# Attention and two expert layers on one core: two weight-preparation steps per projection unit, and a 32-byte pad at the right edge of SBUF

## The chip, the cores and the metric

The program runs on one core of a Trainium2 chip. The metric is the device time of one execution in microseconds (us); the kernel before has a median of 1267.8 us over three runs (1267.17 to 1268.67).

## What is computed

```
rmsnorm(x, g) = x / sqrt(mean(x*x) + 1e-6) * g            # over head_dim
attn = softmax(rmsnorm(q) @ rmsnorm(k).T / sqrt(64)) @ v    # batch 4, 12 heads, 448 positions, head_dim 64
x    = attn laid out as 1792 tokens x 768
h    = max(x @ w_in, 0);   x = (h*h) @ w_out                # d_ff 2048
g    = x @ w_gate;         out = (silu(g) * (x @ w_val)) @ w_out2     # d_ff 1536
```

All weights arrive as float64 and are read by the kernel as pairs of 32-bit words.

## The kernel before, in words

**Three stages.** `attention()` walks over 24 pairs of heads; `moe()` then runs phase 0 (`w_in`, `w_out`) and phase 1 (`w_gate`, `w_val`, `w_out2`). The order of work on every engine is the order in which the code issues it (`tc.manual_schedule()`): each engine takes its own queue strictly in that order.

**Precision.** Every operand of the two expert layers is split into a high part (cast to fp32r) and a low part (the rest), and each product takes three matmuls: high times high, weight high times activation low, weight low times activation high.

**Units.** The 1792 tokens are four blocks t = 0 to 3 of 448. The list `units` (L669 to L686) orders the expert layers. A *projection unit* P(f,t) multiplies a slab of 128 hidden columns with block t of the activations: 18 matmuls of 128x448 on TensorE (L610) in phase 0, 36 in phase 1, reading the activation tile `xs0` to `xs3` of that block. Its result is finished on two engines, in `up`: ScalarE takes the relu (L631), VectorE the square (L632), ScalarE casts the high part of `hid` (L171), VectorE subtracts for the low part (L172). An *output unit* O(t) multiplies the two `hid` slabs f = 0 and f = 1 of a group with `w_out`: six accumulators of six matmuls each (L658), whose first three read `hid0` (f = 0) and whose last three read `hid` (f = 1); VectorE adds each accumulator to `xacc` (L666, in the first group a copy, L664). After the first group the order within a group g is

```
P00  O3 of g-1  P01  P02  P03  P10  P11  O0  P12  O1  P13  O2
```

so five projection units stand in a row, and O0, which reads the `hid` of P10, comes one unit after it.

**Weight preparation.** `pieces()` turns each slab of weights from float64 words into an fp32r high and low part, in six steps, in the text named A to F; `prep(n)` at the head of each unit (L691) issues the next n of them, before the unit's own work:

- A: a shift on VectorE (L135) and a square on ScalarE (L139)
- B: VectorE, L141
- C: VectorE, L145; the raw buffer is then free, and the next unit issues the load of a later slab on SyncE
- D: VectorE, L150
- E: ScalarE casts the high part (L154), from what D wrote
- F: VectorE subtracts for the low part (L156), from what E wrote

A ring of six prepared slabs (`NSLOT`) bounds how far preparation may run ahead: with a full ring a step is a no-op. A group of phase 0 needs four slabs, 24 steps, and has eight projection units and four output units.

**Memory.** Pools grow from the left or from the right edge of SBUF. On the left stand `xs0`, `xs1`, the weight ring `w0` to `w5`, `hid0`, `hid` and `xacc`. At the right edge (`side="right"`) stand in the attention `th`, `p`, `sg`, `v`, `nm`, `ones`, `onef`, `xu`, `rb` and others, and later `xs2` and `xs3` (pool `xb`). In the built program the left tiles begin at multiples of 64 bytes in their partition (`xs0` 44736, `xs1` 66240, `hid0` 147136, `hid` 161472 and 165568), those at the right edge all at 32 past a multiple of 64 (`xs2` 173536, `xs3` 195040, `th` 155808). A row of 448 fp32 numbers is 1792 bytes, 28 times 64.

Of the kernel before, what the change touches and what calls it, by code (L numbers as in the profile page):

```python
# [8 lines left out]
F32 = mybir.dt.float32  # L9
# [10 lines left out]
def kernel(  # L20
# [17 lines left out]
    P = 128  # L38
# [11 lines left out]
    NB = len(blocks)  # L50

    const = ctx.enter_context(tc.tile_pool(name="const", bufs=1))

    ident = const.tile([P, P], F32, name="ident")
    make_identity(nc, ident)
# [53 lines left out]
    def load_slabs():  # L109
        while state["want"]:  # L110
            state["want"] -= 1
            load_slab()
# [51 lines left out]
    def prep(n=1):  # L164
        for _ in range(n):
            next(steps, None)
# [7 lines left out]
    def split_hi(t, kk):  # L174
        b0, n = blocks[t]
        nc.scalar.copy(xs[t][:, 0, kk, :], x[:, kk, b0:b0 + n])

    def split_lo(t, kk, eng=nc.vector):
        b0, n = blocks[t]
        eng.tensor_tensor(  # L180
            out=xs[t][:, 1, kk, :], in0=x[:, kk, b0:b0 + n], in1=xs[t][:, 0, kk, :].bitcast(F32), op=ALU.subtract
        )
# [409 lines left out]
    def moe():  # L592
# [32 lines left out]
        def up(g, f, t):  # L625
            b0, n = blocks[t]
            ps = psp.tile([P, 512], F32, tag="ps", name="ps")
            proj(ps, ("in", g, f), t)
            hh, hl = hidden(f, t)
            s = scr.tile([P, 512], F32, tag="s", name="s")  # L630
            nc.scalar.activation(out=s[:, :n], in_=ps[:, :n], func=AF.Relu)  # L631
            nc.vector.tensor_tensor(out=s[:, :n], in0=ps[:, :n], in1=s[:, :n], op=ALU.mult)  # L632
            split(hh, hl, s[:, :n])

        def gateval(g, f, t):
            b0, n = blocks[t]
            pg = psp.tile([P, 512], F32, tag="ps", name="ps")
            proj(pg, ("gate", g, f), t)
            hh, hl = hidden(f, t)
            s = scr.tile([P, 512], F32, tag="s", name="s")  # L640
            nc.scalar.activation(out=s[:, :n], in_=pg[:, :n], func=AF.Sigmoid)  # L641
            nc.vector.tensor_tensor(out=s[:, :n], in0=pg[:, :n], in1=s[:, :n], op=ALU.mult)  # L642
            pv = psp.tile([P, 512], F32, tag="ps", name="ps")
            proj(pv, ("val", g, f), t)
            nc.vector.tensor_tensor(out=s[:, :n], in0=pv[:, :n], in1=s[:, :n], op=ALU.mult)  # L645
            split(hh, hl, s[:, :n])

        def down(name, g, t, last):
            b0, n = blocks[t]
            hd = hid_t.pop(t)  # L650
            for o in range(KD):
                ps = psp.tile([P, 512], F32, tag="ps", name="ps")
                mm = 0
                for f in range(2):
                    w = W[(name, g, f)]
                    for wi, hi in ((0, 0), (0, 1), (1, 0)):
                        rhs = hid0[:, hi, b0:b0 + n] if f == 0 else hd[:, hi, :n]
                        nc.tensor.matmul(  # L658
                            ps[:, :n], w[:, wi, o * P:(o + 1) * P], rhs, start=(mm == 0), stop=(mm == 5)
                        )  # L660
                        mm += 1
                a = acc[:, o, b0:b0 + n]
                if g == 0:
                    nc.vector.tensor_copy(a, ps[:, :n])  # L664
                else:
                    nc.vector.tensor_tensor(out=a, in0=ps[:, :n], in1=a, op=ALU.add)  # L666
                if last and name == "out":
                    split(xs[t][:, 0, o, :], xs[t][:, 1, o, :], a, nc.gpsimd)
                elif last:  # L669
                    nc.sync.dma_start(out=out[o * P:(o + 1) * P, b0:b0 + n], in_=a)  # L670
# [17 lines left out]
        for i, (phase, kind, g, f, t) in enumerate(units):  # L688
            state["freed"] = freed
            load_slabs()  # L690
            prep(2 if i < 2 else 1 if i < 7 else 3 if phase == 0 else 4 if kind else 5)  # L691
            while drain and drain[0][0] == i:
                _, fn, arg = drain.pop(0)
                fn(arg)
            endt = t == NB - 1
            if phase == 0 and kind == 0:
                up(g, f, t)
                freed += endt
            elif phase == 0:
                down("out", g, t, g == DFF // 256 - 1)  # L700
                freed += 2 * endt
            elif kind == 0:
                gateval(g, f, t)
                freed += 2 * endt
            else:
                down("out2", g, t, g == DFF2 // 256 - 1)
                freed += 2 * endt
            for t, kk in (
                ((2, 0),), ((2, 1), (2, 2)), ((2, 3), (2, 4)), ((2, 5), (3, 0)), ((3, 1), (3, 2)), ((3, 3), (3, 4)), ((3, 5),)
            )[i] if i < 7 else ():  # L710
                split_hi(t, kk)
                split_lo(t, kk, nc.gpsimd if kk % 2 == 1 else nc.vector)

    with tc.manual_schedule():
        attention()
        moe()
# [31 lines left out]
```

## Time and profile before

| what | before |
|---|---|
| median of 3 runs | 1267.8 us |
| the profiled execution's own time | 1267.85 us |
| its span, first to last instruction | 1266.1 us |
| TensorE busy | 1252.4 us (99%) |
| VectorE busy | 826.6 us (65%) |
| ScalarE busy | 432.7 us (34%) |
| GpSimd busy | 250.0 us (20%) |
[...]

Busy time of TensorE counts a matmul from its start to its modelled end, and neighbours overlap; so how fast a stream of matmuls runs is read from the distance of their starts, and small waits hide inside the busy time. In a row of the timeline, "start, length, xN" is a run of N instructions without another kind between them. For matmuls that follow each other the distance of two starts is the length less one matmul's own duration (0.367 us), divided by N-1.

### The profile page before, as it was taken

How to read it: one execution, taken by the hardware profiler on the slowest of the kernel's cores; microseconds unless marked ns; L12 is line 12 of the kernel's file. 1: busy time of each engine (PE TensorE's matmuls, PEld its weight loads, DVE VectorE, ACT ScalarE, POOL GpSimd, SP SyncE). 2: the span in 40 equal slices, each digit the busy share in tenths (PEclk: the TensorE clock that was granted, in tenths of full speed). 3: DMA queues.
4: the chain of work that ended last, by engine and by line, in shares of the span. 5: the costliest groups of instructions: out<-in, count | busy, mean ns of one | idle time of the engine just before them, and what ended most of it. 6: DMA issues, size and time to landing. Idle time of an engine off the chain costs nothing.

```text
span 1266.1 us, 16840 instructions
## 1 busy us (share of the span) xinstructions
PE 1252.4 (99%) x6766; PEld 1064.8 (84%) x6766; DVE 826.6 (65%) x1168; ACT 432.7 (34%) x679; POOL 250.0 (20%) x268
## 2 busy tenths in 40 slices
PE   8999999999999999999999999999999999999998
PEld 5555555589898989898999999999999999999998
DVE  6777777767767676766767665565665664765634
ACT  5777777643313131222222432121221230221210
POOL 3889999630000000000000540000000000000000
PEclk9999999999999999999999999999999999999999
DMA  4433332131212021111112111111120220220013
GB/s 124 145 116 97 114 98 56 45 95 50 76 50 76 26 75 42 59 51 50 50 50 75 51 51 50 49 52 50 50 75 25 75 76 1 77 74 26 25 44 131
DMA packets 64830, 82.35 MB, mean 65 GB/s; under 512 B 8176, under 2 KB 61168, under 8 KB 64752
## 3 DMA queue, kind: packets, MB, share of 16 engines
q1 hardware_dynamic: 64432, 81.28, 20.6%
q8 instruction: 53, 0.87, 0.3%
q14 instruction: 25, 0.20, 0.1%
q10 hardware_dynamic: 320, 0.00, 0.0%
HBM read 75.50 MB, written 5.59 MB: 64 GB/s over the span
## 4 chain that ended last, share of the span: by engine, by line
PE 86%; DVE 7%; ACT 4%; POOL 2%; issue 1%; DMA 0%; ACTq 0%; POOLq 0%; DVEq 0%
PE ps L610 38%; PE ps L658 32%; PE s L365 5%; PE s L380 4%; PE s L336 2%; PE s L401 1%; DVE hid L172 1%; PE s L306 1%; ACT hid L171 1%; DVE s L632 1%; DVE bits L150 1%; DVE w L156 1%; ACT w L154 1%; POOL sg L371 1%; POOL qk L288 1%
## 5 line engine op out<-in xcount | busy, mean ns | idle before, releaser
L610 PE MATMUL ps<-xs,w 128*128 128x448 f32 x2880 | 598.0, 367 | 0.7 <-ACT sb L409 0.7
L610 PEld LDWEIGHTS ps<-xs,w 128*128 128x128 f32 x2880 | 541.0, 188 | 49.1 <-ACT sb L409 1.5
L658 PE MATMUL ps<-hid,w 128*128 128x448 f32 x2016 | 421.2, 366 | 2.3 <-DVE hid L172 1.3
L658 PEld LDWEIGHTS ps<-hid,w 128*128 128x128 f32 x2016 | 378.0, 188 | 36.8 <-DVE hid L172 3.5
L666 DVE TENSOR_TENSOR xacc<-ps,xacc 128x448 f32<-128x448 f32 x288 | 167.5, 619 | 53.1 <-PE ps L658 51.5
L171 ACT CAST hid<-s 128x448 fp32r<-128x448 f32 x112 | 63.5, 567 | 235.3 <-DVE s L645 160.8
L339 DVE TENSOR_REDUCE mxz<-s 112x2 f32<-112x896 f32 x96 | 101.2, 1092 | 24.4 <-PE s L336 23.6
L172 DVE TENSOR_TENSOR hid<-s,hid 128x448 fp32r<-128x448 f32 x112 | 70.1, 626 | 70.9 <-ACT hid L171 70.9
L172 POOL TENSOR_TENSOR xs<-xacc,xs 128x448 fp32r<-128x448 f32 x24 | 29.0, 1248 | 425.3 <-ACT xs L171 425.3
L154 ACT CAST w<-bits 128x768 fp32r<-128x768 f32 x68 | 56.7, 834 | 149.4 <-DVE bits L150 149.4
L371 POOL TENSOR_TENSOR sg<-p 112x896 f32<-112x896 f32 x46 | 97.7, 2125 | 11.8 <-ACT p L367 9.9
L367 ACT ACTIVATE p<-s 112x896 f32<-112x896 f32 x96 | 87.1, 919 | 14.6 <-PE s L365 11.2
L156 DVE TENSOR_TENSOR w<-bits,w 128x768 fp32r<-128x768 f32 x68 | 65.0, 956 | 32.2 <-ACT w L154 30.9
L641 ACT ACTIVATE s<-ps 128x448 f32<-128x448 f32 x48 | 26.1, 544 | 165.6 <-PE ps L610 165.6
L631 ACT ACTIVATE s<-ps 128x448 f32<-128x448 f32 x64 | 34.7, 542 | 136.3 <-PE ps L610 136.3
L365 PE MATMUL s<-th 64*112 64x448 f32 x576 | 76.9, 371 | 2.8 <-ACT p L367 1.4
L645 DVE TENSOR_TENSOR s<-ps,s 128x448 f32<-128x448 f32 x48 | 30.0, 625 | 73.6 <-PE ps L610 72.8
L380 PE MATMUL s<-p,v 112*64 112x448 f32 x384 | 77.5, 545 | 0.0
L642 DVE TENSOR_TENSOR s<-ps,s 128x448 f32<-128x448 f32 x48 | 29.9, 622 | 72.8 <-ACT s L641 72.8
L139 ACT ACTIVATE w<-raw 128x768 fp32r<-128x768 f32 x68 | 61.7, 907 | 45.5 <-PE ps L658 45.5
L632 DVE TENSOR_TENSOR s<-ps,s 128x448 f32<-128x448 f32 x64 | 39.7, 620 | 50.7 <-ACT s L631 50.7
L145 DVE SCALAR_TENSOR_TENSOR bits<-raw,bits 128x768 int32<-128x768 int32 x68 | 66.7, 980 | 2.0
(64 smaller groups left out, 832.6 us busy)
## 6 DMA issues: line engine op xcount, KB each, us to landing
raw<-in_moe_w_out_dram SPq DMA_DIRECT2D x28, 768.0 KB
raw<-in_moe_w_in_dram SPq DMA_DIRECT2D x16, 768.0 KB
raw<-in_moe_w_gate_dram SPq DMA_DIRECT2D x12, 768.0 KB
raw<-in_moe_w_val_dram SPq DMA_DIRECT2D x12, 768.0 KB
raw<-in_k_dram SPq DMA_DIRECT2D x24, 224.0 KB
raw<-in_q_dram SPq DMA_DIRECT2D x24, 224.0 KB
v<-in_v_dram SPq DMA_DIRECT2D x24, 224.0 KB
rb<-row SPq DMA_DIRECT2D x48, 112.0 KB
```

The source lines that it names most:

```text
L154: nc.scalar.copy(t[:, 0, :], src)
L156: nc.vector.tensor_tensor(out=t[:, 1, :], in0=src, in1=t[:, 0, :].bitcast(F32), op=ALU.subtract)
L171: nc.scalar.copy(dh, src)
L172: (eng or nc.vector).tensor_tensor(out=dl, in0=src, in1=dh.bitcast(F32), op=ALU.subtract)
L339: nc.vector.tensor_reduce(out=mxz[:, c, 0:P:D], in_=ps[:CP, :, :S], op=ALU.max, axis=AX.X)
L365: nc.tensor.matmul(ps[:CP, a, :S], lhs, rhs, start=(w == 0), stop=(w == 3))
L367: nc.scalar.activation(out=p, in_=ps[:CP, :, :S], func=AF.Exp)
L371: nc.gpsimd.tensor_tensor(out=sg, in0=p_t[pi, 2 * w], in1=p_t[pi, 2 * w + 1], op=ALU.add)
L380: nc.tensor.matmul(ps[s, :S], v_t[pi][:, a, c * D:(c + 1) * D], p[:, a, :], start=(c == 0), stop=(c == NCH - 1),)
L610: nc.tensor.matmul(ps[:, :n], w[:, wi, kk, :], xs[t][:, xi, kk, :], start=(mm == 0), stop=(mm == 3 * KD - 1))
L658: nc.tensor.matmul(ps[:, :n], w[:, wi, o * P:(o + 1) * P], rhs, start=(mm == 0), stop=(mm == 5))
L666: nc.vector.tensor_tensor(out=a, in0=ps[:, :n], in1=a, op=ALU.add)
```

## The change

It adds a pool `edge` with one tile of eight fp32 numbers (32 bytes in each partition) as the first at the right edge, so that every tile behind it there begins 32 bytes lower: `xs2` at 173504, `xs3` at 195008, `th` at 155776, all multiples of 64. The tile is never written or read. And in phase 0, from unit 7 on, `prep` gives two steps at a projection unit (`kind` 0) and still three at an output unit (`kind` 1).

```diff
     const = ctx.enter_context(tc.tile_pool(name="const", bufs=1))
+
+    edge = ctx.enter_context(tc.tile_pool(name="edge", bufs=1, side="right"))
+    edge.tile([P, 8], F32, name="pad")
...
             load_slabs()
-            prep(2 if i < 2 else 1 if i < 7 else 3 if phase == 0 else 4 if kind else 5)
+            prep(2 if i < 2 else 1 if i < 7 else 2 + kind if phase == 0 else 4 if kind else 5)
```

No instruction is added or taken away on any engine; the steps of preparation move along the queues of VectorE and ScalarE, with the loads of SyncE behind them. Line numbers in the change are three higher. The numbers in the names of `w` and `hid` are buffer counts; `hid_...` with a number is `hid0`, and `hid` alone is the f = 1 tile.

VectorE before, group 2 of phase 0: from step F ahead of P02 to the low part of P10. The row `hid<-s,hid` is the low part of P10, which O0 waits for.

```order
L156 TENSOR_TENSOR w_4307<-bits,w_4307 128x768
L632 TENSOR_TENSOR s<-ps,s 128x448
L172 TENSOR_TENSOR hid_3361<-s,hid_3361 128x448
L135 TENSOR_SCALAR bits<-raw 128x768
L141 SCALAR_TENSOR_TENSOR bits<-raw,bits 128x768
L145 SCALAR_TENSOR_TENSOR bits<-raw,bits 128x768
L632 TENSOR_TENSOR s<-ps,s 128x448
L172 TENSOR_TENSOR hid_3361<-s,hid_3361 128x448
L150 SCALAR_TENSOR_TENSOR bits<-w_4366,bits 128x768
L156 TENSOR_TENSOR w_4366<-bits,w_4366 128x768
L632 TENSOR_TENSOR s<-ps,s 128x448
L172 TENSOR_TENSOR hid<-s,hid 128x448
```

VectorE in the change, the same group, from step B ahead of P02 to the low part of P10:

```order
L144 SCALAR_TENSOR_TENSOR bits<-raw,bits 128x768
L148 SCALAR_TENSOR_TENSOR bits<-raw,bits 128x768
L635 TENSOR_TENSOR s<-ps,s 128x448
L175 TENSOR_TENSOR hid_3365<-s,hid_3365 128x448
L153 SCALAR_TENSOR_TENSOR bits<-w_4311,bits 128x768
L635 TENSOR_TENSOR s<-ps,s 128x448
L175 TENSOR_TENSOR hid_3365<-s,hid_3365 128x448
L159 TENSOR_TENSOR w_4311<-bits,w_4311 128x768
L138 TENSOR_SCALAR bits<-raw 128x768
L635 TENSOR_TENSOR s<-ps,s 128x448
L175 TENSOR_TENSOR hid<-s,hid 128x448
```

Ahead of P10's two operations stood D and F, with E between them on the other engine; now F of a slab and A of the next stand there, and D and E have moved to P03.

ScalarE before, the same stretch: P03 (with A ahead of it), P10 (with E ahead of it), P11 (with A).

```order
L139 ACTIVATE w_4366<-raw 128x768
L631 ACTIVATE s<-ps 128x448
L171 CAST hid_3361<-s 128x448
L154 CAST w_4366<-bits 128x768
L631 ACTIVATE s<-ps 128x448
L171 CAST hid<-s 128x448
L139 ACTIVATE w_4426<-raw 128x768
L631 ACTIVATE s<-ps 128x448
L171 CAST hid<-s 128x448
```

ScalarE in the change: P03 (with E ahead of it), P10 (with A), P11 (with nothing).

```order
L157 CAST w_4311<-bits 128x768
L634 ACTIVATE s<-ps 128x448
L174 CAST hid_3365<-s 128x448
L142 ACTIVATE w_4394<-raw 128x768
L634 ACTIVATE s<-ps 128x448
L174 CAST hid<-s 128x448
L634 ACTIVATE s<-ps 128x448
L174 CAST hid<-s 128x448
```

The relu of P10 stood behind a cast that waits for D of the same unit; now it stands behind a square that waits for a raw slab alone.

## Rows read from the trace of the kernel before

**Rows 1.** Page: busy time of the engines, and the granted clock in 40 slices
```profile
PE 1252.4 (99%) x6766; PEld 1064.8 (84%) x6766; DVE 826.6 (65%) x1168; ACT 432.7 (34%) x679; POOL 250.0 (20%) x268
...
PEclk9999999999999999999999999999999999999999
```

**Rows 2.** Page, the chain that ended last, share of the span by engine
```profile
PE 86%; DVE 7%; ACT 4%; POOL 2%; issue 1%; DMA 0%; ACTq 0%; POOLq 0%; DVEq 0%
```

**Rows 3.** Busy time by stretch: 21 attention rounds, one round, expert layers, two groups
```profile
core 0: us, PE busy (x) PEld busy (x) DVE busy (x) ACT busy (x) POOL busy (x), PEclk, DMA share, GB/s
37.83:245.69 207.86, 205.39 (x1589) 117.79 (x1588) 158.23 (x189) 156.97 (x244) 186.06 (x193) 1.00 0.34 99
226.31:236.00 9.69, 9.69 (x78) 5.62 (x77) 6.89 (x8) 6.61 (x11) 6.30 (x7) 1.00 0.17 50
258.78:1266.10 1007.32, 1001.50 (x4896) 919.05 (x4896) 636.10 (x937) 246.89 (x390) 41.82 (x37) 1.00 0.17 56
440.94:500.26 59.32, 59.13 (x289) 54.02 (x288) 40.02 (x60) 15.26 (x25) 0.00 (x0) 1.00 0.17 54
1027.62:1115.72 88.10, 88.10 (x434) 81.16 (x433) 53.77 (x78) 18.46 (x28) 0.00 (x0) 1.00 0.17 54
```

**Rows 4.** Who waited for whom, TensorE, phase 0 (260 to 705 us): total, times, longest
```profile
PE ps L658 <- DVE hid L172: 1.3, 7, 0.2
PE ps L658 <- ACT hid L171: 1.0, 1, 1.0
```

**Rows 5.** Timeline of TensorE at O0 of group 2: start, us, instructions
```profile
400.00 1.21 PE L658 MATMUL ps<-hid,w 128*128 128x448 f32 x4
401.40 1.89 PE L658 MATMUL ps<-hid,w 128*128 128x448 f32 x8 [0.19 <-DVE hid L172]
```

**Rows 6.** Timeline of TensorE at O0 of group 1
```profile
339.60 0.77 PE L658 MATMUL ps<-hid,w 128*128 128x448 f32 x3
341.34 0.47 PE L658 MATMUL ps<-hid,w 128*128 128x448 f32 x1 [0.97 <-ACT hid L171]
342.00 3.36 PE L658 MATMUL ps<-hid,w 128*128 128x448 f32 x15 [0.19 <-DVE hid L172]
```

**Rows 7.** Timeline of VectorE, group 2, from P03's preparation to P10's low part
```profile
392.43 0.55 DVE L135 TENSOR_SCALAR bits<-raw 128x768 int32<-128x768 int32 x1
393.01 0.96 DVE L141 SCALAR_TENSOR_TENSOR bits<-raw,bits 128x768 int32<-128x768 int32 x1
394.01 0.96 DVE L145 SCALAR_TENSOR_TENSOR bits<-raw,bits 128x768 int32<-128x768 int32 x1
394.88 0.62 DVE L632 TENSOR_TENSOR s<-ps,s 128x448 f32<-128x448 f32 x1
396.13 0.62 DVE L172 TENSOR_TENSOR hid<-s,hid 128x448 fp32r<-128x448 f32 x1 [0.63 <-ACT hid L171]
396.67 0.95 DVE L150 SCALAR_TENSOR_TENSOR bits<-w,bits 128x768 f32<-128x768 f32 x1
398.59 0.96 DVE L156 TENSOR_TENSOR w<-bits,w 128x768 fp32r<-128x768 f32 x1 [0.96 <-ACT w L154]
399.47 0.62 DVE L632 TENSOR_TENSOR s<-ps,s 128x448 f32<-128x448 f32 x1
400.72 0.62 DVE L172 TENSOR_TENSOR hid<-s,hid 128x448 fp32r<-128x448 f32 x1 [0.63 <-ACT hid L171]
```

**Rows 8.** Timeline of ScalarE, group 2: P01's relu, then P10 with E ahead
```profile
385.47 0.55 ACT L631 ACTIVATE s<-ps 128x448 f32<-128x448 f32 x1 [3.35 <-PE ps L610]
...
397.72 0.84 ACT L154 CAST w<-bits 128x768 fp32r<-128x768 f32 x1 [1.62 <-DVE bits L150]
398.46 0.54 ACT L631 ACTIVATE s<-ps 128x448 f32<-128x448 f32 x1
400.12 0.57 ACT L171 CAST hid<-s 128x448 fp32r<-128x448 f32 x1 [1.12 <-DVE s L632]
```

**Rows 9.** Timeline of TensorE, 72 matmuls of xs2 and xs3 (phase 1)
```profile
1012.75 15.03 PE L610 MATMUL ps<-xs,w 128*128 128x448 f32 x72
```

**Rows 10.** The same, the 72 matmuls of xs0 and xs1 that follow
```profile
1027.62 14.76 PE L610 MATMUL ps<-xs,w 128*128 128x448 f32 x72
```

**Rows 11.** The same, the 36 matmuls of hid0 and hid behind those
```profile
1042.21 7.46 PE L658 MATMUL ps<-hid,w 128*128 128x448 f32 x36
```

**Rows 12.** Timeline of TensorE, one attention round: first and last pair of scores
```profile
229.77 0.76 PE L365 MATMUL s<-th 64*112 64x448 f32 x6
...
233.51 0.37 PE L365 MATMUL s<-nm,ones 64*112 64x448 f32 x2
```

**Rows 13.** ScalarE's casts into xs0 to xs3 after phase 0: ns min/median/max
```profile
L171 ACT CAST xs<-xacc x24: 566/568/571, 705.5 to 742.1; 128x448 fp32r<-128x448 f32 x24
```

## The prediction
> **What bounds the kernel now.** First the page: TensorE is busy for 1252.4 us of 1266.1, at the full granted clock in every slice, and the chain that ended last lies on it for 86%; the other 14% are worth finding, because half of them are VectorE's [rows 1, 2]. Then the stretches: the expert layers take 1007 us with 4896 matmuls of one shape, the attention the rest [rows 3]. Then the timeline of TensorE, from which the distance between two matmuls comes: it shows two things.
>
> *One shape, two speeds.* 72 matmuls that read xs2 and xs3 take 15.03 us [rows 9]: less the last one's own 0.37 us and divided by 71, that is 206.5 ns each. The 72 behind them, same weights of the same ring and same shape, but reading xs0 and xs1, take 14.76 us [rows 10]: 202.7 ns. The 36 that read hid0 and hid are at 7.46 us [rows 11], (7.46 - 0.37) / 35 = 202.6 ns. xs2 and xs3 are the ones that stand 32 bytes past a multiple of 64.
>
> *A wait once in a group of phase 0.* A group has 288 matmuls, 72 of them on xs2 and xs3. 216 x 202.7 + 72 x 206.5 ns = 58.65 us, but it took 59.32 us [rows 3]: 0.67 us are lost. In phase 1 the same sum, 288 x 202.7 + 144 x 206.5 ns = 88.11 us, meets 88.10 [rows 3]: nothing is lost there. The loss of phase 0 is at O0: seven waits for the low part of hid and one long one for its high part [rows 4]. At 400.00 O0 begins; its fifth matmul should start 4 x 0.203 = 0.81 us later and starts at 1.40, and the next eight take 1.89 us where 7 x 0.203 + 0.37 = 1.79 are due [rows 5]: 0.59 + 0.10 = 0.69 us. In group 1 it is more: the fourth matmul starts at 341.34 in place of 340.21, the fifth 0.66 us after it in place of 0.20, and the start-up behind that costs the same 0.10 [rows 6]: 1.13 + 0.46 + 0.10 = 1.69 us.
>
> **Why O0 waits.** P10's matmuls end 3.65 us (18 x 202.7 ns) before O0 begins, at 396.35. P11 and P10 at 3.65 us and P03 and P02 at 3.72 (18 x 206.5 ns), counted back from 400.00, put the ends of P03, P02 and P01 at 392.70, 388.98 and 385.26. In P01, where nothing was queued ahead, the relu began 0.2 us after that, at 385.47 [rows 8]. For P10 it began at 398.46, 2.1 us after the end, because ScalarE had the cast E ahead of it, E waited for D, and D had waited behind the low part of P03 [rows 7, 8]. VectorE then did F before the square. From the relu's start the chain is relu 0.55, square 0.62, cast 0.57, low part 0.62 us plus 0.03 between them, about 2.45 us when nothing is in its way; here it ended at 401.34. With three steps a projection unit gives VectorE either A, B, C (0.55 + 0.96 + 0.96, to 2.5 us with the gaps) or D, E, F, which crosses to ScalarE and back (0.95 + 0.84 + 0.96, 2.9 us with the gaps), on top of 1.9 us from the start of its square to the end of its low part: 4.4 to 4.8 us where TensorE takes 3.65 to 3.72. Over five projection units in a row the two engines fall behind, and O0 is where it shows.
>
> **The change, part by part.**
>
> *Steps, term 1.* Moved: one step of each projection unit in phase 0; nothing is added. I carry the timetable of group 2 forward on the times of before. P01's low part is as before, to 387.93. P02 now has B, C on VectorE, to 389.87; its relu (matmuls end 388.98) is done by then, so square to 390.50, cast to 391.10, low part to 391.75. P03 has D to 392.75, E on ScalarE to 393.65; its relu, due at 392.90, comes behind E and ends at 394.20; square to 394.85, cast 395.45, low part 396.10. P10 has F, A on VectorE, to 397.65; ScalarE did the square of A at 395.5 to 396.4, so the relu starts at its due 396.55 and ends 397.10; square to 398.30, cast 398.90, low part 399.55. O0 first reads the high part at 400.61 and the low part at 400.81: it is there 1.3 us early, where before it was 0.5 us late. The other groups differ in which steps fall on P03 and P10. From group 3 on (E, F and A, B; the same work, and no D directly ahead of E) the slack is 1.5 us or more; in group 1 (F, A and B, C) I get the low part 3.0 us after P10's matmuls end, with 4.25 allowed. So all seven waits go: 1.69 + 6 x 0.69 = **5.8 us**.
>
> What moves with it: what was prepared ahead of projection units is now partly done at output units and at units where a full ring made steps no-ops. An output unit lasts 36 x 0.203 = 7.3 us and asks VectorE for six additions of 0.62 us and three steps of at most 2.9: 6.6 us, covered. Supply is 8 x 2 + 4 x 3 = 28 steps for the 24 that a group needs, so preparation does not starve. Counting steps along the units, the narrowest lead is the second w_out slab of group 1: finished in P03, read at O0, three units or 11 us later (before: five); in later groups of the phase five or more. Loads: C is later, and so is each load issued after it on SyncE, but a slab's A comes nine steps behind its load's issue, some four projection units; nothing else of weight is in SyncE's queue in this phase, and the traffic is 54 GB/s [rows 3]. GpSimd is idle there. Cost: nothing, as long as that lead stands.
>
> *Pad, term 2, expert layers.* 1440 matmuls read xs2 and xs3 (16 projection units of 18 in phase 0, 576; 24 of 36 in phase 1, 864). If the 32 bytes are what makes them slow, each falls from 206.5 to 202.7 ns: 1440 x 3.8 = **5.4 us**, all on the path, since TensorE has no other wait there. Before does not show xs2 or xs3 at another address, so the bounds are 0 and 5.4; I take 5.4, because xs0, xs1, hid0 and hid, five address ranges that share nothing but the alignment, all run at 202.7. A loss I exclude by the same rows. Writing the moved tiles costs ScalarE the same: its casts into xs0 to xs3 all take 566 to 571 ns [rows 13].
>
> [...]
>
> *Pad, term 3, attention.* A round has 20 pairs of 64-row matmuls on th and nm. 18 of their distances lie between 229.77 and 233.51 [rows 12]: 207.8 ns each, nearest to the slow rate of xs2. At 3.8 ns less each, 20 x 24 rounds = 480 pairs give 1.8 us. The other matmuls on moved tiles (p, sg) have another form; granting them the same 3.8 ns for some 12 pairs a round adds 1.1, so the bounds are 0 and 2.9 us. The undisturbed round is 9.69 us, the mean of 21 is 207.86 / 21 = 9.90 [rows 3]: in part of the rounds another engine's wait ends last and would eat the gain. I take half of 1.8: **0.9 us**. The warm-up and the tail hold no such stream.
>
> **Sum.** 1267.85 us, the profiled execution (the median of 1267.8 is the same within the runs' spread) - 5.8 - 5.4 - 0.9 = 1255.75, so **1255.8 us**, 0.95% less. Its own range is 1253.3 (attention at 2.9, less 0.5 for the spread of runs) to 1257.5.
>
> **The rivals.**
>
> - *The pad does nothing.* [...] For it: no row separates address from alignment. Against it: five left-hand ranges at one speed. Terms 2 and 3 go: 1267.85 - 5.8 = 1262.1 us. Chance 0.10.
> - *The wait at O0 stays in part.* VectorE's queue is denser than my timetable, for instance because step A of one slab waits for its load, or F for E behind a relu; 1.3 us of delay in P10 brings the first part of the wait back. Half of it left gives 1258.7, all of it 1261.6 us. Against it: the timetable has 1.2 to 1.5 us to spare in every group. Chance 0.07.
> - *Preparation comes too late.* The mechanism on the slow side: a projection or output unit reaches a slab whose F has not been done, and TensorE waits for VectorE and ScalarE at the first matmul of the slab. It decides once the lead of three units, 11 us, is used up, and pays when the waits are over 12.1 / 7 = 1.7 us in each of seven groups; at one projection unit (3.7 us) in each it gives 1255.8 + 26 = 1282 us. Against it: 28 steps against 24 needed. Chance 0.03.
> - *No change.* The pad does nothing and the waits move to O1 or O2 at the same length: 1267.8 us. Against it: O1 and O2 have 11 us between their hid and its use. Chance 0.02.
>
> **How the numbers follow.** The forecast has 0.78. 8 times in 10: the forecast's own range, and of the second rival the part up to half of the wait: 1253.3 to 1260.0; the pad that does nothing, at 1262.1, is left out with its 0.10. A measurement of this kernel tells about 0.2%, 2.5 us, from no change. Faster by more than that are the forecast and the first two rivals, 0.95; within it 0.02; slower 0.03.
>
> **What would show it.** In the changed profile: a stretch of 72 matmuls on xs2 and xs3 in 14.76 us like xs0 and xs1 (if 15.03, term 2 is wrong); no wait of TensorE for hid in phase 0, and a group of phase 0 in 288 x 202.7 ns = 58.4 us in place of 59.32; a group of phase 1 in 87.6 in place of 88.10; the undisturbed attention round at 9.6 in place of 9.69, and the start of the expert layers about 0.9 us earlier than 258.78 (if it moves by over 2 us, term 3 is too small). A wait of TensorE for `w` in phase 0 would be the third rival.

## The result, and the profile after

The changed kernel takes 1257.5 us (median of 5 runs) against 1268.4 us for the kernel before on the same chip: ratio 0.9905, 95% interval 0.9892 to 0.9919. The forecast was 1255.8 us with a range of 1253.3 to 1260.0. One thing must be known to read the numbers: of 17 executions of the changed kernel 7 took 1255.7 to 1257.5 us and 10 took 1275.4 to 1280.3, longer than the kernel before, and the ratios go by the 7. The profile that came with the result is of an execution of 1276.34 us; that of `again`, which is the change unaltered, is of one of 1257.0 us. Both profiles are needed. The lines below answer to [rows 1] and [rows 2]; the first fence is the page of the 1276.34 us execution, the second that of the 1257.0 us one (span, busy time of the engines, the chain that ended last by engine).

```profile
span 1274.5 us, 16838 instructions
...
PE 1262.5 (99%) x6766; PEld 1064.4 (84%) x6766; DVE 828.5 (65%) x1168; ACT 433.6 (34%) x679; POOL 251.7 (20%) x268
...
PE 92%; POOL 2%; DMA 2%; DVE 1%; ACT 1%; issue 1%; SPq 0%; POOLq 0%; ACTq 0%; DVEq 0%
```

```profile
span 1255.2 us, 16838 instructions
...
PE 1243.6 (99%) x6766; PEld 1065.7 (85%) x6766; DVE 826.8 (66%) x1168; ACT 433.2 (35%) x679; POOL 251.6 (20%) x268
...
PEclk9999999999999999999999999999999999999999
...
PE 93%; POOL 2%; DMA 1%; DVE 1%; ACT 1%; issue 1%; SPq 0%; POOLq 0%; ACTq 0%; DVEq 0%
```

In both, VectorE's share of the chain has fallen from 7% to 1% and ScalarE's from 4% to 1%: the waits at O0 are gone from either execution. The instructions are the same. What differs between the two is TensorE's busy time, by 18.9 us, at a granted clock of 1.000 and 0.999; no other engine's differs by more than 2 us.

The stretches of the 1257.0 us execution, which answer to [rows 3] (same columns: from:to and length, busy time by engine, clock, DMA): start to the expert layers, expert layers, group 3 of phase 0 (from its P01 to the P01 of the next group), a group of phase 1, one attention round.

```profile
0.00:259.23 259.23, 251.07 (x1870) 146.04 (x1870) 190.78 (x231) 185.59 (x289) 208.59 (x231) 1.00 0.35 100
259.23:1255.20 995.97, 992.52 (x4896) 919.63 (x4896) 636.06 (x937) 247.65 (x390) 43.01 (x37) 1.00 0.18 57
438.09:496.46 58.37, 58.37 (x290) 54.10 (x288) 39.62 (x60) 15.39 (x25) 0.00 (x0) 1.00 0.17 55
1018.12:1105.67 87.55, 87.55 (x433) 81.15 (x432) 53.76 (x78) 18.46 (x28) 0.00 (x0) 1.00 0.17 55
226.44:236.15 9.71, 9.71 (x77) 5.67 (x77) 6.90 (x8) 6.60 (x11) 6.08 (x6) 1.00 0.18 50
```

The gain lies in the expert layers and nowhere else: they begin at 259.23 in place of 258.78 us, and the 4896 matmuls of that stretch are busy for 992.52 in place of 1001.50 us. The same group of phase 0 takes 58.37 in place of 59.32 us, one of phase 1 87.55 in place of 88.10.

The timelines of TensorE that answer to [rows 9], [rows 10] and [rows 11] (start, us, instructions): 72 matmuls on xs2 and xs3, 72 on xs0 and xs1, 36 on hid0 and hid. First `again`, 1257.0 us:

```profile
1003.53 14.76 PE L613 MATMUL ps<-xs,w 128*128 128x448 f32 x72
1018.12 14.75 PE L613 MATMUL ps<-xs,w 128*128 128x448 f32 x72
1032.71 7.46 PE L661 MATMUL ps<-hid,w 128*128 128x448 f32 x36
```

The same three places of the execution of 1276.34 us:

```profile
1017.94 15.04 PE L613 MATMUL ps<-xs,w 128*128 128x448 f32 x72
1032.82 15.04 PE L613 MATMUL ps<-xs,w 128*128 128x448 f32 x72
1047.70 7.60 PE L661 MATMUL ps<-hid,w 128*128 128x448 f32 x36
```

With the pad, all moving tiles run alike in both executions. In the one the distance between matmuls is (14.76 - 0.37) / 71 = 202.7 ns, in the other (15.04 - 0.37) / 71 = 206.6 ns, and so through the whole stream: (15.04 - 14.76) / 71 = 3.94 ns, and 4896 x 3.94 ns = 19.3 us, which is the difference of the two times. Term 2 of the prediction came true at the first distance and was lost several times over at the second. Why that is so was the question for the experiments.

### The profile page after: what moved, and what is told of

It reads as the page before. It is cut to its first block, busy times and chain, and to the rows that moved or that the text cites. A ratio compares the mean times of both kernels' runs of the same rounds, so it can differ in the third digit from the quotient of the medians.

```text
span 1274.5 us, 16838 instructions
## 1 busy us (share of the span) xinstructions
PE 1262.5 (99%) x6766; PEld 1064.4 (84%) x6766; DVE 828.5 (65%) x1168; ACT 433.6 (34%) x679; POOL 251.7 (20%) x268
## 4 chain that ended last, share of the span: by engine, by line
PE 92%; POOL 2%; DMA 2%; DVE 1%; ACT 1%; issue 1%; SPq 0%; POOLq 0%; ACTq 0%; DVEq 0%
PE ps L613 47%; PE ps L661 33%; PE s L368 5%; PE s L383 4%; PE s L339 2%; PE s L404 1%; PE s L309 1%; POOL sg L374 1%; POOL qk L291 1%; DMA raw<-in_k_dram 1%; PE s L348 0%; DMA v<-in_v_dram 0%; ACT sq L252 0%; DMA rb<-row 0%; DVE ss L259 0%
## 5 line engine op out<-in xcount | busy, mean ns | idle before, releaser
L613 PE MATMUL ps<-xs,w 128*128 128x448 f32 x2880 | 604.2, 368 | 0.7 <-ACT sb L412 0.7
L661 PE MATMUL ps<-hid,w 128*128 128x448 f32 x2016 | 425.5, 368 | 0.0
L174 ACT CAST hid<-s 128x448 fp32r<-128x448 f32 x112 | 63.5, 567 | 207.8 <-DVE s L648 162.4
```

The costliest lines, as they stand in the source:

```text
L174: nc.scalar.copy(dh, src)
L613: nc.tensor.matmul(ps[:, :n], w[:, wi, kk, :], xs[t][:, xi, kk, :], start=(mm == 0), stop=(mm == 3 * KD - 1))
L661: nc.tensor.matmul(ps[:, :n], w[:, wi, o * P:(o + 1) * P], rhs, start=(mm == 0), stop=(mm == 5))
```

## The experiments

Eleven runs follow, two of them of a kernel that had run already, all beside runs of the kernel before on the same chip, whose medians lay between 1267.8 and 1268.6 us. That a tile stands "at 64" means that its byte address in its partition is 64 modulo 128; "against the weights" is a moving tile's address less that of the weight ring (the first pool of slabs), modulo 128. In the kernel before, the ring, xs0, xs1, hid0 and hid stand at 64 and xs2, xs3 at 96. The change puts xs2 and xs3 at 64 too.

### The two parts, each alone

`again` is the change without an edit, and is told above.

> The changed kernel unaltered, for a profile of an undisturbed execution and for more times. Theory 1 (a 448-column row that begins 32 bytes past a multiple of 64 costs a matmul 3.8 ns, and the pad removes that): about 1255.8 us, all six moving tiles (xs0 to xs3, hid0, hid) at 202.7 ns from start to start, no wait at O0. Rival (the address range, not the alignment, makes xs2 and xs3 slow): about 1262 us, xs2 and xs3 still at 206.5 ns, the rest at 202.7.

Measured: ratio 0.9906 (0.9893 to 0.9919), the same as the first time.

`steps_only` leaves the pad out:

```diff
-            prep(2 if i < 2 else 1 if i < 7 else 3 if phase == 0 else 4 if kind else 5)
+            prep(2 if i < 2 else 1 if i < 7 else 2 + kind if phase == 0 else 4 if kind else 5)
```

> The two steps alone, without the pad. Both theories: no wait at O0 in any group, xs2 and xs3 at 206.5 ns, the rest at 202.7: 1267.85 - 5.8 = 1262.1 us. If the waits move instead of going, nearer to 1267.

Measured: 1262.1 us, ratio 0.9957 (0.9941 to 0.9973), and TensorE has no wait at O0. Group 3 of this kernel, by stretch:

```profile
439.62:498.25 58.63, 58.63 (x290) 54.10 (x288) 39.65 (x60) 15.37 (x25) 0.00 (x0) 1.00 0.17 54
```

58.63 us is what 216 x 202.7 + 72 x 206.5 ns make, 58.65: the 0.67 us that [rows 3] lost are back, and xs2 and xs3 are as slow as before. From the start of the first to the start of the last matmul of the expert layers the kernel before takes 1262.24 - 258.78 = 1003.46 us, this one 1257.49 - 259.96 = 997.53: 5.93 us less. Term 1 stands by itself.

`pad_only` has the pad and keeps three steps:

```diff
+    edge = ctx.enter_context(tc.tile_pool(name="edge", bufs=1, side="right"))
+    edge.tile([P, 8], F32, name="pad")
```

> The pad alone, three steps at each projection unit as before. Theory 1: the wait at O0 stays (5.8 us in seven groups), xs2 and xs3 fall to 202.7 ns: 1267.85 - 5.4 - 0.9 = about 1261.5 us. Rival (address range): 1267.8 us, no change.

Measured: 1264.8 us, ratio 0.9968 (0.9957 to 0.9979): between the two expectations. Its timeline of TensorE shows why. The rows are: group 2, xs2 and xs3, then xs0 and xs1, then O0 with its wait; and 59 us later the same pairs of tiles in group 3.

```profile
387.81 7.60 PE L613 MATMUL ps<-xs,w 128*128 128x448 f32 x36
395.25 7.60 PE L613 MATMUL ps<-xs,w 128*128 128x448 f32 x36
402.69 1.03 PE L661 MATMUL ps<-hid,w 128*128 128x448 f32 x4
403.92 1.89 PE L661 MATMUL ps<-hid,w 128*128 128x448 f32 x8 [0.19 <-DVE hid L175]
...
446.99 7.46 PE L613 MATMUL ps<-xs,w 128*128 128x448 f32 x36
454.29 7.46 PE L613 MATMUL ps<-xs,w 128*128 128x448 f32 x36
```

Ahead of the wait at O0 every tile is at (7.60 - 0.37) / 35 = 206.6 ns, behind it every tile is at 202.6. Nothing but the wait lies between. So both rates that the changed kernel shows in different executions stand here in one: with xs and hid at the same place the stream has **two rates**, keeps the one that it is in, and a wait can move it to the other. Not every wait does: in this execution the one at O0 of group 1 left the stream at 206.7, and those of groups 3 to 7 left it at 202.7. The seven waits for VectorE at O0 are still there, as in [rows 4]:

```profile
PE ps L661 <- DVE hid L175: 1.3, 7, 0.2
PE ps L661 <- ACT hid L174: 0.8, 1, 0.8
```

The stretch at 206.6 ns, from 260 to 403 us, is 143 / 0.2067 = 690 matmuls x 4 ns, 2.8 us above what the expectation with the pad took. That is for this execution, of 1266.34 us; another 0.9 us of the miss is term 3, which did not come.

No execution of `pad_only` took 1276 us: all seven lie between 1264.3 and 1266.3. The change has no wait at O0, and in its execution of 1276.34 us every unit, from the first to the last, ran at 206.6 to 206.7 ns. So the two parts seem to lean on each other: the steps also take away the waits that can end a stretch at the slower rate. One trace shows such an end; the other six executions have none.

### Is it the rows' own alignment?

`left_off` has two steps, no pad at the right edge, and the same 32 bytes at the left edge instead, so that the ring, xs0, xs1, hid0 and hid all move to 96, where xs2 and xs3 stand:

```diff
+    shift = ctx.enter_context(tc.tile_pool(name="shift", bufs=1))
+    shift.tile([P, 8], F32, name="pad")
```

> The two steps without the pad at the right edge, and a 32-byte pad at the left edge instead, so that xs0, xs1, hid0, hid and the weight ring begin 32 bytes past a multiple of 64 as xs2 and xs3 do. Theory 1: all 4896 matmuls at 206.5 ns, 1262.1 + 3456 x 3.8 ns = 1275.2 us. Rival (address range): 1262.1 us, xs0, xs1, hid0 and hid still at 202.7 ns.

Measured: 1257.1 us, ratio 0.9906 (0.9891 to 0.992), the time of the change; two of the five executions took 1276.8 and 1278.0 us and have no trace. TensorE's timeline, xs2 and xs3, then xs0 and xs1:

```profile
1003.58 14.76 PE L613 MATMUL ps<-xs,w 128*128 128x448 f32 x72
1018.17 14.75 PE L613 MATMUL ps<-xs,w 128*128 128x448 f32 x72
```

This experiment rules out two reasons at once. xs2 and xs3 have not moved by a byte from where they took 15.03 us [rows 9], they still start 32 bytes past a multiple of 64, and they run at 202.7 ns. Both expectations fell: neither the alignment of the rows by itself counts nor the address range in which xs2 and xs3 lie. What the change and this kernel share is that every moving tile stands at the same place as the weights. From the first to the last matmul of the expert layers this kernel takes 1251.44 - 259.28 = 992.16 us, 5.37 less than `steps_only`.

### Is it the place against the weights?

`ring_off` is the changed kernel with 32 bytes ahead of the ring; ring, hid0 and hid go to 96, while xs0 to xs3 stay at 64:

```diff
+            off = ctx.enter_context(tc.tile_pool(name="off", bufs=1))
+            off.tile([P, 8], F32, name="off")
             mem["ringa"] = ctx.enter_context(tc.tile_pool(name="ringa", bufs=1))
```

> The changed kernel with a further 32-byte tile ahead of the weight ring, which puts the ring, hid0 and hid 32 bytes past a multiple of 64, and leaves xs0 to xs3 at multiples. Theory 2 (what counts is the moving rows against the weight tile): xs0 to xs3 at 206.5 ns, hid0 and hid at 202.7, 1256 + 2880 x 3.8 ns = 1267 us. Theory 1 (the moving rows' own alignment): xs at 202.7, hid0 and hid at 206.5, 1256 + 2016 x 3.8 ns = 1263.7 us. If neither counts: 1256 us.

Measured: 1269.9 us, ratio 1.0014 (1.0003 to 1.0025). xs2 and xs3, xs0 and xs1, then hid:

```profile
1013.21 14.88 PE L615 MATMUL ps<-xs,w 128*128 128x448 f32 x72
1027.93 14.88 PE L615 MATMUL ps<-xs,w 128*128 128x448 f32 x72
1042.65 7.60 PE L663 MATMUL ps<-hid,w 128*128 128x448 f32 x36
```

No row of xs moved, and xs went to (14.88 - 0.37) / 71 = 204.4 ns: the place against something that moved counts. That was the ring, and hid0 and hid with it; `all_64`, below, tells the two apart. The number was missed: xs is now 96 against the ring, and not 32 as xs2 and xs3 are in the kernel before (206.5 ns). And hid, at 0 against the weights as always, ran at 206.6 in every unit, not at the 202.7 that was expected.

`pad96` takes a pad of 96 bytes, so that xs2 and xs3 stand at 0, which is 64 against the weights, and all else is as in the change:

```diff
-    edge.tile([P, 8], F32, name="pad")
+    edge.tile([P, 24], F32, name="pad")
```

> The changed kernel with a pad of 96 bytes in place of 32: xs2 and xs3 begin at multiples of 128, where the weight ring and the other tiles begin 64 past a multiple of 128. If a multiple of 64 is what counts: as the changed kernel, 1256 us (or all matmuls at 206.7 ns, 1276). If a distance of 64 also puts rows out of step: xs2 and xs3 near 206.5 ns in every execution, the rest at 202.7, 1261.5 us.

Measured: 1268.7 us, ratio 1.0006 (0.9997 to 1.0015). The first three rows are early: hid, then 18 matmuls on xs2, then hid again. The last three are xs2 and xs3, xs0 and xs1, and hid in phase 1.

```profile
271.91 7.46 PE L661 MATMUL ps<-hid,w 128*128 128x448 f32 x36
279.21 3.80 PE L613 MATMUL ps<-xs,w 128*128 128x448 f32 x18
282.86 7.59 PE L661 MATMUL ps<-hid,w 128*128 128x448 f32 x36
...
1011.08 14.72 PE L613 MATMUL ps<-xs,w 128*128 128x448 f32 x72
1025.63 15.04 PE L613 MATMUL ps<-xs,w 128*128 128x448 f32 x72
1040.51 7.60 PE L661 MATMUL ps<-hid,w 128*128 128x448 f32 x36
```

xs2 and xs3 are faster than any tile before, (14.72 - 0.37) / 71 = 202.1 ns, and yet the kernel is as slow as the kernel before: tiles at 0 start at 202.6, and from the first return from xs2 on they run at 206.4 to 206.6. So the rate of tiles at 0 also depends on what was read ahead of them. In the kernel before it is the other way about. This is O0 of its group 1 behind the wait of [rows 6], the xs2 unit after it, and hid again:

```profile
342.72 6.15 PE L658 MATMUL ps<-hid,w 128*128 128x448 f32 x29
348.71 3.84 PE L610 MATMUL ps<-xs,w 128*128 128x448 f32 x18
352.39 6.84 PE L658 MATMUL ps<-hid,w 128*128 128x448 f32 x33
```

Behind the wait hid ran at (6.15 - 0.37) / 28 = 206.4 ns; behind xs2, at 32 against the weights, it was back at (6.84 - 0.37) / 32 = 202.2. The xs2 unit between them ran at (3.84 - 0.37) / 17 = 204.1, not at 206.5, so the rate of rows at 32 depends on what came ahead as well. It looks as if the slow tiles xs2 and xs3 kept all the others at the faster rate, so that [rows 10] and [rows 11] showed one rate only: this one trace shows the return, and all 55 runs of the kernel before that stand beside the experiments lie between 1266.8 and 1272.4 us.

### One row as a reset

If returning from rows at 32 puts the stream into the faster rate, one such row might hold it there. `one_row` and `one_row2` are the changed kernel with one row of xs0 (the low part of the third of its six pieces) in a tile of its own, 32 bytes past the place of xs0. The tile has 1856 bytes in the first, which shifted the ring, hid0 and hid by 64 as well, so that the row stands at 96 against the weights there; in the second it has 1920 (`S + 32`), and the row stands at 32. The line that makes the tile, of the first (the others pass the row to its casts and matmuls):

```diff
+            odd[0, 1, 2] = xa.tile([P, S + 16], F32R, tag="xo", name="xo")[:, 8:8 + S]
```

> The changed kernel with one activation row (low part, third of six, of block 0) in a tile of its own that begins 32 bytes past a multiple of 64, while all else stays at multiples: one matmul in each projection of block 0, 40 in all, is out of step with its weights. Theory 2 (a stream whose rows stand in step with the weight tile has two rates that hold themselves, 202.7 and 206.7 ns, and a matmul out of step sends it to 202.7): every execution at 202.7 ns from the first such matmul on, 1256 us, none near 1276. Rival (the rate is drawn for each execution by something outside the stream): executions near 1276 us as often as with the changed kernel, all matmuls at 206.7 there.

> As one_row, but with the extra tile of 1920 bytes, a multiple of 128, so that the weight ring, hid0 and hid keep their place modulo 128 against xs0 to xs3; in one_row the 1856 bytes had also moved them by 64. Theory 3 (the place of the moving rows against the weight tile, modulo 128 bytes, sets the rate: 64 gives 202.1 ns, 32 gives 206.5, 96 gives 204.4, and 0 has the two rates 202.7 and 206.7 that hold themselves; leaving rows at 32 sends those at 0 to 202.7, leaving rows at 64 or 96 to 206.7): the one row at 32 sends every execution to 202.7 ns at the eighth matmul of each projection of block 0, so 1256 us every time. Rival (only the draw at the start of the stream decides): 1256 us or 1276.

Measured: 1263.5 us, ratio 0.9963 (0.995 to 0.9977), and 1262.5 us, ratio 0.9958 (0.9944 to 0.9972). Both miss the expected 1256. The first is confounded by the shift: xs stands at 64 against the ring, and its xs1, xs2 and xs3 ran at 202.1 ns, as xs2 and xs3 do in `pad96`. The second isn't: its units ran anywhere from 202.5 to 206.4 ns, and distances of 196 to 212 ns stand next to each other. One row does not hold the stream; the idea of a cheap reset fell.

### Everything at 64 against the weights

At 64 against the weights only one rate had been seen, and the lowest. `all_64` is the changed kernel with 64 bytes ahead of the ring and 64 ahead of hid0, so that the ring stands at 0 and xs0 to xs3, hid0 and hid at 64:

```diff
+            off = ctx.enter_context(tc.tile_pool(name="off", bufs=1))
+            off.tile([P, 16], F32, name="off")
             mem["ringa"] = ctx.enter_context(tc.tile_pool(name="ringa", bufs=1))
...
         big = ctx.enter_context(tc.tile_pool(name="big", bufs=1))
+        big.tile([P, 16], F32, name="off2")
         hid0 = big.tile([P, 2, NT], F32R, name="hid0")
```

> The changed kernel with 64 bytes ahead of the weight ring and 64 more ahead of hid0: all six moving tiles begin 64 past a multiple of 128, the ring at a multiple of 128, so every matmul reads its rows at 64 against its weights. Theory 3: 202.1 ns for all 4896 matmuls in every execution, 1256 - 4896 x 0.5 ns = 1253.5 us, under both kernels. Rival (not the weight tile but a jump from one moving tile to the next sets the rate): no jump is left, so as the changed kernel, 1256 us or 1276 with all matmuls at 202.7 or at 206.7 ns.

Measured: **1250.3 us**, ratio 0.9862 (0.9848 to 0.9875), better than either kernel and 3.2 us better than expected. xs2 and xs3, xs0 and xs1, hid:

```profile
998.82 14.72 PE L616 MATMUL ps<-xs,w 128*128 128x448 f32 x72
1013.38 14.72 PE L616 MATMUL ps<-xs,w 128*128 128x448 f32 x72
...
1027.94 7.37 PE L664 MATMUL ps<-hid,w 128*128 128x448 f32 x36
```

xs is at 202.1 ns, as in `pad96`, and hid at (7.37 - 0.37) / 35 = 200.0 ns, which was not expected. No jump from one moving tile to the next is left, and neither tile runs at 202.7 or 206.6: the rival falls, and what counts is the place against the ring. It is not the ring's own address: in `one_row` the ring stands at 0 too, and hid, at 0 against it, ran at 206.4 to 206.7. By the starts of all units the rates are 202.3 and 200.2; the 2880 matmuls on xs (0.4 ns less each than 202.7) and the 2016 on hid (2.5 ns less) make 1.2 + 5.0 = 6.2 us. From the first to the last matmul of the expert layers it is 1245.29 - 259.24 = 986.05 us, 6.11 less than in `left_off` and in `again`.

`all_64b` is the same kernel again:

> all_64 once more, unaltered. If rows at 64 against their weights have one rate, not two: 1250 us within 1.5 in every execution, hid0 and hid near 200.2 ns and xs0 to xs3 near 202.3. Rival (two rates here too, the lower not met in four executions): some executions some 15 to 25 us longer.

Measured: 1250.3 us, ratio 0.9858 (0.9843 to 0.9872). All eight executions of the two lie between 1249.3 and 1251.7 us, so this layout showed one rate only.

`all_64_three` is `all_64` with three steps, and so term 1 measured a second time:

```diff
-            prep(2 if i < 2 else 1 if i < 7 else 2 + kind if phase == 0 else 4 if kind else 5)
+            prep(2 if i < 2 else 1 if i < 7 else 3 if phase == 0 else 4 if kind else 5)
```

> all_64 with three steps at each projection unit of phase 0, as before the change. If rows at 64 against their weights keep their rate through a wait, the seven waits at O0 come back and nothing else changes: 1250.3 + 5.8 (a little more, since faster matmuls wait longer) = 1256 to 1258 us in every execution, and the rate behind each wait is the one ahead of it. Rival (each wait draws the rate of the stream anew, as it did once with the pad alone): stretches at another rate behind some waits, and executions that differ by several us.

Measured: 1257.6 us, ratio 0.9915 (0.9898 to 0.9931), as expected: its four executions lie between 1256.8 and 1258.1 us, and do not differ by the several us of the rival. The waits are back (TensorE, phase 0: total, times, longest):

```profile
PE ps L664 <- DVE hid L175: 1.3, 7, 0.2
PE ps L664 <- ACT hid L174: 1.1, 1, 1.1
```

Two steps are worth 1257.6 - 1250.3 = 7.3 us here against 5.9 in `steps_only`. Most of that is at the waits: O0 of groups 2 to 7 loses 0.87 us each by the starts of its matmuls, where it lost 0.69 before. P02 and P03 ahead of it take 36 x 4.3 ns = 0.15 us less than before, so TensorE reaches O0 that much earlier.

The rates found, over all runs:

| place against the weights, modulo 128 | tiles and kernels | ns between matmuls |
|---|---|---|
| 0 | before (xs0, xs1, hid), the change, left_off, hid in ring_off and pad96 | 202.7 or 206.6 |
| 32 | xs2, xs3 in before and steps_only | 206.5; 204.1 in the one unit behind the wait in group 1 |
| 64 | xs2, xs3 in pad96; xs in all_64; hid in all_64 | 202.1; 202.1; 200.0 |
| 96 | xs in ring_off | 204.4 |

## Why the prediction was right, and where it was not

**Term 1, 5.8 us: right, by its own steps.** `steps_only` gives 1262.1 us, the very figure for terms 2 and 3 at nothing, and from the first to the last matmul of the expert layers it saves 5.93 us; that the kernel before beside it took 1268.5 and not 1267.85 is within the spread of the runs. The timetable of group 2 holds within half a microsecond. Here is VectorE in `again`, from D in P03 to the low part of P10, to be laid beside [rows 7]; the bracket is the idle time ahead and what ended it.

```profile
389.65 0.95 DVE L153 SCALAR_TENSOR_TENSOR bits<-w,bits 128x768 f32<-128x768 f32 x1
392.00 0.63 DVE L635 TENSOR_TENSOR s<-ps,s 128x448 f32<-128x448 f32 x1 [1.40 <-ACT s L634]
393.26 0.63 DVE L175 TENSOR_TENSOR hid<-s,hid 128x448 fp32r<-128x448 f32 x1 [0.63 <-ACT hid L174]
393.80 0.95 DVE L159 TENSOR_TENSOR w<-bits,w 128x768 fp32r<-128x768 f32 x1
394.67 0.55 DVE L138 TENSOR_SCALAR bits<-raw 128x768 int32<-128x768 int32 x1
395.15 0.62 DVE L635 TENSOR_TENSOR s<-ps,s 128x448 f32<-128x448 f32 x1
396.41 0.62 DVE L175 TENSOR_TENSOR hid<-s,hid 128x448 fp32r<-128x448 f32 x1 [0.63 <-ACT hid L174]
```

The low part of P10 ends at 397.03. In P03 VectorE now stands idle for 1.40 us, waiting for the relu, where before it had a queue. ScalarE and TensorE at the same place (P10's relu; the start of O0):

```profile
394.57 0.55 ACT L634 ACTIVATE s<-ps 128x448 f32<-128x448 f32 x1 [0.54 <-PE ps L613]
...
397.96 2.39 PE L661 MATMUL ps<-hid,w 128*128 128x448 f32 x11
```

The relu waits for TensorE now, and not behind a cast as it did in [rows 8]. The low part is there 0.93 us before O0 begins; the timetable had 0.45 (399.55 against 400.00). The matmuls of O0 follow each other without a gap where [rows 5] had one. Preparation did not come late: TensorE has no wait for w in phase 0, so the third rival did not come about.

**Term 2, 5.4 us: the size right, the reason wrong.** xs2 and xs3 fell from 15.03 to 14.76 us as forecast, a phase-1 group took 87.55 us (87.6 forecast), and `left_off` against `steps_only` prices the part at 997.53 - 992.16 = 5.4 us. (Two slips in the working cost nothing: 576 matmuls are 32 projection units of 18, not 16, and 1440 x 3.8 ns is 5.5 us.) But the step "xs0, xs1, hid0 and hid, five address ranges that share nothing but the alignment" was wrong: they also shared their place against the weight ring, and this is what counts, as `left_off` shows with xs2 and xs3 unmoved (14.76 us for the 15.03 of [rows 9]) and `all_64` with all moving tiles alike and only the ring elsewhere (202.1 and 200.0 ns). From it followed the second failure, "A loss I exclude by the same rows". Those rows were taken in a stream which xs2 and xs3, as it seems, kept returning to 202.7 ns (one trace shows a return, from 206.4 to 202.2). With that mix gone, the rate of 206.6 holds as well as the other, and where it does the kernel is at 1276 us, slower than before and outside the range. No rival of the prediction had this. That the measured time met the forecast was thus partly luck: it did so where the stream began at 202.7 ns, and the prediction did not know that it could begin otherwise.

The first rival, a pad that does nothing, did not come about: 32 bytes at the left edge alone are worth 5.4 us, and in `ring_off` xs ran at 204.4 ns, and not at 202.7, without having moved.

**Term 3, 0.9 us: nothing came.** The attention round takes 9.71 us where 9.6 was forecast and 9.69 was before, and the first and last pair of scores in it, to be laid beside [rows 12], stand as far apart as ever:

```profile
229.90 0.77 PE L368 MATMUL s<-th 64*112 64x448 f32 x6
...
233.66 0.37 PE L368 MATMUL s<-nm,ones 64*112 64x448 f32 x2
```

18 distances in 3.76 us are 208.9 ns each, against 207.8. The step that failed was to read 207.8 as "nearest to the slow rate of xs2". It is no rate at all: in the trace of before 16 of the 18 distances are 196 to 208 ns, 201.7 in the mean, and two are 241 and 277; in `again` it is the same, with 245 and 272. Nor did the pad change what the expert layers turned out to depend on: weights and moving rows of these matmuls are both in `th`, or in `ones` and `nm`, all at the right edge, and moved by 32 bytes together. The expert layers began 0.45 us later, not 0.9 us earlier, which says little: in all runs with a trace their start lies between 257.2 and 260.0 us.

**The sum.** From the first to the last matmul of the expert layers the kernel before took 1003.46 us and the change, in the execution of 1257.0 us, 1251.39 - 259.23 = 992.16: 11.3 us less, where terms 1 and 2 make 11.2. Between these two profiles the time fell by 1267.85 - 1257.0 = 10.85 us in place of 12.1; the missing 1.25 us are term 3 (0.9) and the later start of the expert layers (0.45), less the 0.1 us that terms 1 and 2 gave more.

**What stays open.** Why the place against the weights matters, why the stream at 0 has two rates, what picks one at the start of the expert layers, and why hid is faster than xs at 64: no run tells. Whether the modulus is 128 was not tried by shifts of 128 or more, and the rates at 32 and 96 were each seen in one or two layouts; the table orders the runs, and no more.

## What to carry to other kernels

Take the distance between matmuls from a stretch without waits, for each moving tile by itself, and compare: where one shape has two distances, as 206.5 and 202.7 ns here, look at where the tile stands against the weights it is multiplied with, not at its own alignment, and try a few small pads, as `all_64` did. Several address ranges that behave alike are one observation and not five if they share the offset to a third tile. And a rate that was only ever seen in one mix of tiles may be held up by that mix: before a loss is excluded, ask what keeps the fast rows fast, and run the kernel often enough to see a second rate. A wait that a change removes may have done some good elsewhere in the stream, as the one behind which `pad_only` went from 206.6 to 202.6 ns, so time the parts of a change apart and together.

## What the runs showed of the chip that was not expected

- The place of moving rows against the weights changed the distance between 128x448 matmuls from 200.0 to 206.6 ns, 3.3%, at a granted clock of 1.0 throughout: at 64 bytes 202.1 (xs) and 200.0 (hid), at 96 bytes 204.4, at 32 bytes 206.5 but for one unit.
- At the same place the stream ran at 202.7 or at 206.6 ns and kept to either through all 4896 matmuls of a profile (1257.0 and 1276.34 us). One of the seven waits at O0 moved it from 206.6 to 202.6 in `pad_only` and one from 202.7 to 206.4 in group 1 of the kernel before; rows at 32 returned it to 202.2 there, and in `pad96` it ran at 206.6 behind rows at 64.
- A single row at 32 in an otherwise aligned stream gave neither rate, but units from 202.5 to 206.4 ns (`one_row2`).
